# Attention and mixture of experts on one core: rebuilding the attention stage (casting loads, crossbar transposes, a softmax laid out by 32x32 block transposes)

## The chip, the cores and the metric

The kernel runs on one core of a Trainium2 chip. The core has a matrix engine (PE, with its weight loads shown apart as PEld), a vector engine (DVE), a scalar engine (ACT), a general engine (POOL) and a queue engine (SP) that only issues transfers; SP, ACT and POOL each have a queue from which transfers (DMAs) can be issued, and all transfers share 16 DMA engines. The metric is the device time of one execution in microseconds (us). All engines work through their own instructions in the order in which the program lists them.

## The reference

The inputs are `x` (8 batches, 8 heads, 512 tokens, 64 features), `state` (the same with 32 states in place of the tokens), a gate matrix and the two weight matrices of eight experts, all fp32.

```python
def _attn_ref(x, state):
    scores = scale * np.matmul(x, state.transpose(0, 1, 3, 2))
    a = softmax(scores, -1)
    xread = np.matmul(a, state)
    scores2 = scale * np.matmul(state, x.transpose(0, 1, 3, 2))
    a2 = softmax(scores2, -1)
    sread = np.matmul(a2, x)
    return np.concatenate([xread, sread], axis=2)

def _moe_ref(x, w_gate, w1, w2):                 # x: 4352 rows of 512
    logits = x @ w_gate
    P = np.exp(logits - logits.max())
    for _ in range(8):                           # Sinkhorn
        P /= P.sum(1, keepdims=True) + 1e-09
        P /= P.sum(0, keepdims=True) + 1e-09
        P *= N / E
    for e in range(E):
        h = np.maximum(x @ w1[e], 0.0)
        out += P[:, e:e + 1] * (h @ w2[e])
```

So each batch needs two softmaxes of the same 512x32 score matrix per head: along the 32 states (for `xread`) and along the 512 tokens (for `sread`). Every row of the attention output then goes through all eight experts, weighted by P.

## The kernel before, in words

The 4352 rows are nine blocks: one of 512 token rows for each batch, and one of 256 rows with the state reads of all batches. `xread` is never formed: the kernel keeps the token softmax `aT` (4 heads x 32 states on 128 partitions, 512 tokens along the row), and multiplies the small projections V = state @ w1 (`project`, L225, `project_ops`, L709) with it, which gives the hidden layer of a token block directly. The ninth block uses the state reads `xsT`.

The run has two stages.

The first stage holds the attention of all batches, expert 0 for all nine blocks, the Sinkhorn loop and the first hidden layers of expert 1. Its order is not written by hand: every piece is an `Op` with a rank (a due time), a table of engines it may run on with assumed times, the ops that it follows and the buffers it takes and uses. `issue` (L48) is a list scheduler that plays these assumed times through and emits the instructions in the order that results. The due times come from `due_x` (attention unit u), `due_e` (expert 0, block bi) and `due_1` (expert 1), L354 to L356; the assumed costs of the evictions from PSUM are `EVICT16` and `EVICT32`, L358 and L359. All PSUM tiles of this stage come from one ring of eight banks.

The attention works in 16 units: batch b, and in it two groups q of four heads. For a batch, SP loads x in two transfers of 512 KB in fp32 (L444), POOL casts them to fp16 (L451; DVE and ACT for the first batch), PE transposes x against an identity (L512), and ACT or DVE copies each transposed tile out of PSUM (L516). A unit then has:

- the scores twice, once with tokens on the partitions (`psA`, eight products, L537) and once with states on the partitions (`psB`, two products, L543);
- on DVE: the two maxima (L547, L551), a scale (L554), the difference (L558), later the sum and reciprocal (L574, L575) and the normalization of the state softmax (L569, L570);
- on ACT: the two exponentials (L562, L566);
- on POOL: the normalization of the token softmax (L578);
- on PE: the transposes of both softmaxes (L599, L603), each copied out of PSUM by ACT or DVE (L606, L609), and the state reads (L622), copied out in two pieces (L629).

`bdT` holds the transposed states in fp16, in block-diagonal form, prepared from eight small copies (L402) and 16 transposes (L416). The gate product of a block (L648) follows its attention. When all gates are done, the Sinkhorn loop (L669 to L703) runs as a chain of small DVE instructions and one PE product in each of eight rounds. Expert 0 has hidden products L746, their relu (L382, L384), output products L781 and their copy to `acc`. The weights of experts 0 and 1 are loaded in fp32 by SP (L473, L475) into three staging buffers, and cast by ACT or DVE (L480, L482).

The second stage (L875 on) is written by hand: experts 1 to 7, nine blocks each, with the output layer of one block (`layer2`, seven products of a Strassen scheme, L298, and adds on DVE, L312) mixed with the hidden layer of the next (`layer1`, L252 and L271). The weights of the next expert are loaded by SP and cast by ACT, one piece for every sixth step (`load_w`, L159).

Of the kernel before, what the change touches and what calls it, by code (L numbers as in the profile page):

```python
# [35 lines left out]
class Op:  # L36
# [3 lines left out]
    def __init__(self, rank, on, emit, after=(), takes=(), uses=()):  # L40
        self.rank, self.on, self.emit = rank, on, emit
        self.after = [d for d in after if d is not None]
        self.takes, self.end = list(takes), None
        for slot in list(takes) + list(uses):
            slot.users.append(self)


def issue(ops):  # L48
# [8 lines left out]
    while ready:  # L57
        best = None
        for op in ready:
            at = max([d.end for d in op.after], default=0.0)  # L60
            for slot in op.takes:
                t = slot.ring.free_at()
                at = None if at is None or t is None else max(at, t)
            if at is None:
                continue
            for eng, (busy, late) in op.on.items():
                start = max(at, free.get(eng, 0.0))
                key = (round(start, 2), op.rank, start + late)
                if best is None or key < best[0]:
                    best = (key, op, eng, start, busy, late)  # L70
# [7 lines left out]
        free[eng] = start + busy  # L78
        op.end = start + late
# [8 lines left out]
def kernel(  # L88
# [37 lines left out]
        tc.tile_pool(name="psum", bufs=8, space=bass.MemoryType.PSUM))}  # L126
# [13 lines left out]
    make_identity(nc, ident32)  # L140
    ones128 = persist.tile([128, 128], FP32, name="ones128")
    nc.vector.memset(ones128, 1.0)
    wg_st = persist.tile([128, NKC, E], FP32, name="wg_st")
    wgh = persist.tile([128, NKC, E], FP16, name="wgh")
    bdT = persist.tile([128, B, NQ, 128], FP16, name="bdT")
# [8 lines left out]
    mwst = ctx.enter_context(tc.tile_pool(name="moe_wst", bufs=3))  # L154
# [4 lines left out]
    def load_w(e, engines):  # L159

        w1h = mw.tile([128, NKC, F], FP16, name="w1h", tag="w1h")
        w2h = mw.tile([128, NFB, Dm], FP16, name="w2h", tag="w2h")
        w16[e] = (w1h, w2h)
        casts = []
        n = NKC + NFB // 2
        for k in range(n + 2):
            if k < n:
                if k < NKC:
                    st = mwst.tile([128, F], FP32, name="w1st", tag="wst")
                    nc.sync.dma_start(out=st, in_=w1r[e, :, k, :])  # L170
                    casts.append((w1h[:, k, :], st))
                else:
                    g = k - NKC
                    st = mwst.tile([128, 2, Dm], FP32, name="w2st", tag="wst")
                    nc.sync.dma_start(out=st, in_=w2r[e, :, ds(g * 2, 2), :])
                    casts.append((w2h[:, ds(g * 2, 2), :], st))
            if k >= 2:
                dst, src = casts[k - 2]
                eng = engines[(k - 2) % len(engines)]
                if eng is nc.scalar:  # L180
                    nc.scalar.copy(out=dst, in_=src)  # L181
                else:
                    eng.tensor_copy(out=dst, in_=src)
            yield
        if e:

            while not tpool:
                yield
            T = tpool[0].tile([128, 4, NJ, DH], FP16, name="T", tag="T")
            tsum[e] = T  # L190
            b11, b12 = w2h[:, :NJ, :DH], w2h[:, :NJ, DH:]
            b21, b22 = w2h[:, NJ:, :DH], w2h[:, NJ:, DH:]
            for i, (p, q) in enumerate(((b12, b11), (b22, T[:, 0]), (b22, b12), (b21, T[:, 1]))):
                for g in range(2):
                    jj = ds(g * (NJ // 2), NJ // 2)
                    nc.vector.tensor_sub(T[:, i, jj], p[:, jj], q[:, jj])  # L196
                    yield
# [7 lines left out]
    axs = actx.enter_context(tc.tile_pool(name="attn_xs", bufs=2))  # L205
    axp = actx.enter_context(tc.tile_pool(name="attn_x", bufs=3))
    axt = actx.enter_context(tc.tile_pool(name="attn_xt", bufs=2))
    asb = actx.enter_context(tc.tile_pool(name="attn_sb", bufs=2))
    spl = actx.enter_context(tc.tile_pool(name="stprep", bufs=1))

    def gate(bi):
        t0, tn = blocks[bi]
        n = tn // 128
        ps = bank([128, 4, E], FP32, "gate_ps")
        for i in range(n):
            rows = ds(i * 128, 128)
            if bi < B:
                terms = [(aT[:, bi, q, rows], G[:, bi, q]) for q in range(NQ)]
            else:
                terms = [(xsT[:, kc, rows], wgh[:, kc, :]) for kc in range(NKC)]  # L220
            for k, (lhs, rhs) in enumerate(terms):
                nc.tensor.matmul(ps[:, i], lhs, rhs, start=(k == 0), stop=(k == len(terms) - 1))
        nc.scalar.copy(out=logits[:, ds(t0 // 128, n)], in_=ps[:, :n])

    def project(e, bi):  # L225
# [5 lines left out]
        for f in range(F // 512):  # L231
            cols = ds(f * 512, 512)
            ps = [bank([128, 512], FP32, "v_ps", ring[0]) for _ in range(NQ)]
            for j in range(4):
                for q in range(NQ):
                    r = ((j ^ q) % 2) * 64
                    nc.tensor.matmul(ps[q][ds(j * Ns, Ns), :], bdT[ds(r, 64), bi, q, ds(j * Ns, Ns)],  # L237
# [116 lines left out]
    due_x = lambda u: 10.0 + 5.54 * u  # L354
    due_e = lambda bi: 25.1 + 13.7 * bi
    due_1 = 150.0  # L356
    rings = {"bank": Ring(8)}
    EVICT16 = {"DVE": (0.36, 0.48), "ACT": (0.50, 0.66)}  # L358
    EVICT32 = {"ACT": (0.50, 0.66), "DVE": (0.62, 0.74)}  # L359
    engines = {"DVE": nc.vector, "ACT": nc.scalar, "POOL": nc.gpsimd}  # L360

    def op(rank, on, emit, after=(), takes=(), uses=()):
        o = Op(rank, on, emit, after, takes, uses)
# [22 lines left out]
    def dma(rank, kb, emit, after=(), takes=()):  # L386
        return op(rank, {"DMA": (kb / 330.0, kb / 330.0 + 2.2)}, lambda _: emit(), after, takes)


    st_bd = spl.tile([128, B, NQ, 128], FP16, name="st_bd")  # L390
    nc.vector.memset(st_bd, 0.0)
    st_st = spl.tile([128, B, NQ, D], FP32, name="st_st")
    bd = []
    for q in range(NQ):
        for j in range(4):
# [5 lines left out]
            def place(eng, q=q, j=j):  # L401
                copy(eng, st_bd[ds(j * Ns, Ns), :, q, ds(((j ^ q) % 2) * D, D)],  # L402
                     st_st[ds(j * Ns, Ns), :, q])

            bd.append(op((0, 0), {"DVE": (0.30, 0.40), "POOL": (0.70, 0.80)}, place,
                         [dma((0, 0), 120, load)]))
# [3 lines left out]
    bdT_ready = []  # L410
    for g in range(4):
        ps = psum([128, 4, 128], FP16, "stT_ps")

        def turn(_, g=g, ps=ps):
            for i in range(4):
                nc.tensor.transpose(ps.tile[:, i], st_bd[:, 2 * g + i // 2, i % 2, :], identh)  # L416

        def keep(eng, g=g, ps=ps):
            copy(eng, bdT[:, ds(2 * g, 2)].rearrange("p b q c -> p (b q) c"), ps.tile)

        t = op((0, 1, g), {"PE": (0.35, 0.55)}, turn, bd, [ps])
        bdT_ready.append(op((0, 1, g), EVICT16, keep, [t], uses=[ps]))
    gps = psum([128, B, NQ, E], FP32, "G_ps")

    def gmul(_):
        for b in range(B):
            for q in range(NQ):
                for par in range(2):
                    nc.tensor.matmul(gps.tile[ds(par * 64, 64), b, q], bdT[:, b, q, ds(par * 64, 64)],
                                     wgh[:, 2 * q + par])  # L430

    gm_op = op((20.0,), {"PE": (1.0, 1.2)}, gmul, bdT_ready + [wgc], [gps])
    G_ready = op((20.0,), {"DVE": (0.2, 0.3), "ACT": (0.3, 0.4)},
                 lambda eng: copy(eng, G, gps.tile), [gm_op], uses=[gps])


    xn = [slot(axp, 3, [128, NSC, H, D], FP16, "x_nat") for _ in range(B)]
    x_ready = []
    for b in range(B):
        for g in range(2):  # L440
            st = slot(axs, 2, [128, H // 2, NSC * D], FP32, "x_st")

            def load(b=b, g=g, st=st):
                nc.sync.dma_start(  # L444
                    out=st.tile,
                    in_=x[b, ds(g * 4, 4), :, :].rearrange("h (p sc) d -> p h (sc d)", sc=NSC))

            def cast(eng, b=b, g=g, st=st):
                src = st.tile.rearrange("p h (sc d) -> p sc h d", sc=NSC)
                for sc in range(NSC):  # L450
                    copy(eng, xn[b].tile[:, sc, ds(g * 4, 4), :], src[:, sc])  # L451

            d = dma((0 if b < 1 else due_x(2 * b - 2), b, 0), 512, load, takes=[st])
            on = {"DVE": (0.90, 1.10), "ACT": (1.35, 1.50)} if b == 0 else {"POOL": (1.65, 1.80)}
            x_ready.append(op((0, 3) if b == 0 else (due_x(2 * b - 2),), on, cast, [d] + x_ready[2 * b:],
                              [xn[b]] if g == 0 else [], [st] + ([xn[b]] if g else [])))
# [6 lines left out]
    def weights_ops(e, rank, on):  # L463
# [3 lines left out]
        for k in range(NKC + NFB // 2):  # L467
            first = k < NKC
            st = slot(mwst, 3, [128, F], FP32, "wst")

            def load(k=k, st=st):
                if k < NKC:
                    nc.sync.dma_start(out=st.tile, in_=w1r[e, :, k, :])  # L473
                else:
                    nc.sync.dma_start(out=st.tile.rearrange("p (a b) -> p a b", a=2),  # L475
                                      in_=w2r[e, :, ds((k - NKC) * 2, 2), :])

            def cast(eng, k=k, st=st):
                if k < NKC:
# [455 lines left out]
```

## Time and profile before

| what | value |
|---|---|
| time, median of 3 runs (lowest, highest) | 793.67 us (792.33, 793.72) |
| span of the profiled execution, first to last instruction | 792.9 us |
| what the median lies above that span | 0.8 us (the profile gives no other time for its own execution) |
| PE busy | 764.5 us (96%) |
| DVE busy | 648.8 us (82%) |
| ACT busy | 566.7 us (71%) |
| POOL busy | 39.5 us (5%) |
| moved by DMA | 52.46 MB |

"Busy" is the time in which an instruction of the engine is under way. For PE it is not the same as work at full rate, since products are pipelined and their ends are modelled: what a run of products really costs is read from the start of one group to the start of the next. The same holds for DVE and ACT in a smaller measure: a DVE instruction that reads 512 fp32 values lasts 0.68 us, and the next one starts 0.60 us after it.

### The profile page before, as it was taken

To read this page: it belongs to the slowest core of one execution; us is meant where nothing else is said; L and a number is where in the kernel's file an instruction comes from. 1 tells how busy PE (TensorE), PEld (TensorE's weight loads), DVE (VectorE), ACT (ScalarE), POOL (GpSimd) and SP (SyncE) were. 2 spreads that over 40 slices of the span, in tenths; PEclk is the share of its full clock that TensorE was granted. 3 is DMA by queue.
4 is the path that set the end of the run, shared out by engine and by line. 5 is a ranking of instruction groups with operands and counts; after the bars stand their busy time and mean duration, and the time that the engine had idled before them with its cause. 6 is when DMAs were issued, how large, how long until landed. Compare 5 with 4: busy or idle time off the path is not lost.

```text
span 792.9 us, 16564 instructions
## 1 busy us (share of the span) xinstructions
PE 764.5 (96%) x6593; PEld 514.2 (65%) x6593; DVE 648.8 (82%) x1603; ACT 566.7 (71%) x1072; POOL 39.5 (5%) x80
## 2 busy tenths in 40 slices
PE   4899999989999999999999999999999999999996
PEld 3455554556667666766667666766667766767675
DVE  7898877787898888978788888978788888978885
ACT  5787776568977688577866688578866688576662
POOL 1543210000000000000000000000000000000000
PEclk9999999999999999999999999999999999999999
DMA  8874000002400033001410033001400030002233
GB/s 280 288 253 138 1 2 1 1 1 64 125 28 1 1 104 111 1 2 54 129 33 2 1 107 107 1 2 54 133 28 2 1 107 28 1 24 97 95 107 134
DMA packets 29535, 52.46 MB, mean 66 GB/s; under 512 B 4625, under 2 KB 12817, under 8 KB 29457
## 3 DMA queue, kind: packets, MB, share of 16 engines
q1 hardware_dynamic: 28368, 51.14, 20.3%
q8 instruction: 51, 0.84, 0.4%
q10 hardware_dynamic: 1088, 0.26, 0.2%
q14 instruction: 28, 0.22, 0.1%
HBM read 42.48 MB, written 8.91 MB: 65 GB/s over the span
## 4 chain that ended last, share of the span: by engine, by line
PE 63%; DVE 4%; ACT 2%; issue 0%; DVEq 0%
PE hps L252 22%; PE Bseed L298 16%; PE E L298 11%; PE A L298 10%; PE v_ps L237 3%; DVE acc L312 2%; ACT Hm L271 2%; DVE sm L277 1%; ACT w2h L181 1%; DVE sm L280 0%; DVE Hm L278 0%; DVE T L196 0%; DVE sm L279 0%; ACT w1h L181 0%; DVE acc L320 0%
## 5 line engine op out<-in xcount | busy, mean ns | idle before, releaser
L271 ACT ACTIVATE Hm<-hps 128x512 f16<-128x512 f32 (+1 forms) x488 | 262.3, 575 | 149.8 <-PE hps L252 138.9
L298 PEld LDWEIGHTS <-Hm 128*128 128x128 f16 x1904 | 185.4, 98 | 74.4 <-issue 3.9
L252 PE MATMUL hps<-aT,V 128*128 128x512 f16 x864 | 230.5, 379 | 0.0
L312 DVE SCALAR_TENSOR_TENSOR acc<-Bseed,Pmat,acc 128x256 f32<-128x256 f32 x357 | 156.9, 479 | 57.1 <-PE Bseed L298 53.6
L298 PEld LDWEIGHTS <-sm 128*128 128x128 f16 x1428 | 134.4, 98 | 54.9 <-DVE sm L277 24.4
L298 PE MATMUL Bseed<-T,Hm 128*128 128x256 f16 x952 | 124.5, 273 | 2.7 <-DVE acc L312 2.5
L298 PE MATMUL A<-w2h,Hm 128*128 128x256 f16 x952 | 126.1, 273 | 0.5
L252 PEld LDWEIGHTS <-V 128*128 128x128 f16 x864 | 84.5, 98 | 44.4
L241 ACT CAST V<-v_ps 128x512 f16<-128x512 f32 x216 | 111.0, 608 | 0.0
L312 DVE SCALAR_TENSOR_TENSOR acc<-E,Pmat,acc 128x256 f32<-128x256 f32 x238 | 104.4, 478 | 5.4 <-PE E L298 1.0
L277 DVE TENSOR_TENSOR sm<-Hm 128x512 f16<-128x512 f16 (+1 forms) x122 | 49.9, 409 | 21.6 <-ACT Hm L271 20.8
L298 PE MATMUL E<-T,sm 128*128 128x256 f16 x476 | 64.4, 274 | 0.7
L781 PE MATMUL yps<-w2h,hT 128*128 128x512 f16 x272 | 64.6, 379 | 0.0
L312 DVE SCALAR_TENSOR_TENSOR acc<-A,Pmat,acc 128x256 f32<-128x256 f32 x119 | 52.4, 479 | 15.0 <-PE A L298 14.9
L298 PE MATMUL Bseed<-T,sm 128*128 128x256 f16 x476 | 62.3, 272 | 2.3 <-ACT Bseed L323 2.3
L298 PE MATMUL E<-w2h,sm 128*128 128x256 f16 x476 | 62.3, 273 | 0.0
L278 DVE TENSOR_TENSOR Hm<-Hm 128x512 f16<-128x512 f16 (+1 forms) x122 | 50.0, 410 | 4.2
L280 DVE TENSOR_TENSOR sm<-Hm,sm 128x512 f16<-128x512 f16 (+1 forms) x122 | 50.0, 410 | 4.2
L279 DVE TENSOR_TENSOR sm<-sm,Hm 128x512 f16<-128x512 f16 (+1 forms) x122 | 49.1, 403 | 0.0
L323 ACT COPY Bseed<-A 128x512 f32<-128x512 f32 (+1 forms) x63 | 34.7, 552 | 18.7 <-PE A L298 15.6
L781 PEld LDWEIGHTS <-hT 128*128 128x128 f16 x272 | 24.8, 98 | 27.5 <-issue 2.6
L746 PE MATMUL hps<-aT,V 128*128 128x512 f16 x160 | 41.1, 389 | 0.4
(114 smaller groups left out, 626.1 us busy)
## 6 DMA issues: line engine op xcount, KB each, us to landing
w1st<-in_moe_w_dram SPq DMA_DIRECT2D x24, 512.0 KB, 3.6
w2st<-in_moe_w_dram SPq DMA_DIRECT2D x24, 512.0 KB, 3.6
x_st<-in_x_dram SPq DMA_DIRECT2D x16, 512.0 KB, 5.1
wst<-in_moe_w_dram SPq DMA_DIRECT2D x16, 512.0 KB, 6.1
out_dram<-acc SPq DMA_DIRECT2D x32, 256.0 KB, 3.1
out_dram<-acc SPq DMA_DIRECT2D x8, 64.0 KB, 1.7
st_st<-in_state_dram ACTq DMA_DIRECT2D x4, 64.0 KB, 3.2
st_st<-in_state_dram SPq DMA_DIRECT2D x4, 64.0 KB, 3.0
```

Of the source, the lines that this page charges most:

```text
L241: nc.scalar.copy(out=V[:, q, cols], in_=ps[q])
L252: nc.tensor.matmul(out, lhs, rhs, start=(k == 0), stop=(k == len(terms) - 1))
L271: nc.scalar.activation(out=Hm[:, i, j, :tn], in_=hps[:, :tn], func=AF.Relu)
L277: nc.vector.tensor_add(s1, a21, a22)
L278: nc.vector.tensor_sub(a21, a11, a21)
L279: nc.vector.tensor_sub(s2, s1, a11)
L280: nc.vector.tensor_sub(s4, a12, s2)
L298: nc.tensor.matmul(dst[:, c], lhs(j, c), rhs[:, j], start=first and c == 0 and j == 0, stop=(j == NJ - 1), skip_group_check=True)
L312: nc.vector.scalar_tensor_tensor(out=dst, in0=src[:, c], scalar=p[:, k], in1=dst, op0=ALU.mult, op1=ALU.add)
L323: nc.scalar.copy(out=Bb[:, :nk], in_=A[:, :nk])
L746: nc.tensor.matmul(ps.tile[:, :tn], lhs, rhs, start=(k == 0), stop=(k == len(terms) - 1))
L781: nc.tensor.matmul(yps.tile, hT[fb].tile[:, ds(tk * 128, 128)], w2h[:, fb, :], start=(fb == 0), stop=(fb == NFB - 1))
```

## The change

The attention stage is rebuilt, and the weight loads of the whole kernel change their way.

- **Loads.** x and all expert weights are loaded by DMAs issued from POOL that cast from fp32 to fp16 on the way. The staging buffers and all cast instructions on POOL, ACT and DVE go. The eight loads of `state` stay on SP and ACT, in fp32.
- **Transposed x.** A DMA issued from SP, `dma_start_transpose`, writes the transposed fp16 x of one group of four heads (128 partitions x 1024 values) into `xT`: two a batch. The PE transposes of x and their copies go.
- **One score product.** The scores are formed once, with states on the partitions: eight products on 64x32 tiles of the PE array, 256 columns each, into two PSUM banks of their own (a ring with one place). The other ring has six banks instead of eight.
- **Token softmax.** DVE's `transpose`, which transposes 32x32 blocks, turns the scores into a layout with the 32 states of one token along the row. Maximum, difference, exponential, sum and normalization work there, all but the exponential on DVE, and a second block transpose turns the result into `aT` with no PE transpose and no copy out of PSUM. POOL's normalization goes to DVE.
- **State reads.** 16 products on 128x64 tiles instead of eight, copied out in one piece instead of two.
- **Prepared states.** Two copies instead of eight and a memset; the gate matrix G takes 64 small products on tiles instead of 32.
- **Planner.** New due times and costs; an op can occupy a second engine (`also`), and an alternative can carry a handicap (`SHY`, 0.8 us for fp32 evictions on DVE).

The core of the diff:

```diff
-    def load_w(e, engines):
+    def load_w(e):
...
-                    st = mwst.tile([128, F], FP32, name="w1st", tag="wst")
-                    nc.sync.dma_start(out=st, in_=w1r[e, :, k, :])
-                    casts.append((w1h[:, k, :], st))
...
+        for g in range(2):
+            nc.gpsimd.dma_start(out=w1h[:, ds(2 * g, 2), :], in_=w1r[e, :, ds(2 * g, 2), :])
+        for g in range(2):
+            nc.gpsimd.dma_start(out=w2h[:, ds(NJ * g, NJ), :], in_=w2r[e, :, ds(NJ * g, NJ), :])
+        for _ in range(10):
             yield
...
-    due_x = lambda u: 10.0 + 5.54 * u
-    due_e = lambda bi: 25.1 + 13.7 * bi
-    due_1 = 150.0
-    rings = {"bank": Ring(8)}
-    EVICT16 = {"DVE": (0.36, 0.48), "ACT": (0.50, 0.66)}
-    EVICT32 = {"ACT": (0.50, 0.66), "DVE": (0.62, 0.74)}
+    due_x = lambda u: 6.0 + 4.4 * u
+    due_e = lambda bi: 14.0 + 13.0 * bi
+    due_1 = 135.0
+    rings = {"bank": Ring(6), "pair": Ring(1)}
+    SHY = 0.8
+    EVICT16 = {"DVE": (0.34, 0.48), "ACT": (0.48, 0.66)}
+    EVICT32 = {"ACT": (0.48, 0.66), "DVE": (0.60, 0.74, SHY)}
...
+    xn = [slot(axp, 4, [128, H, NSC * D], FP16, "x_nat") for _ in range(B)]
+    for b in range(B):
+        def load(b=b):
+            for g in range(2):
+                nc.gpsimd.dma_start(
+                    out=xn[b].tile[:, ds(g * 4, 4), :],
+                    in_=x[b, ds(g * 4, 4), :, :].rearrange("h (p sc) d -> p h (sc d)", sc=NSC))
+
+        x_ready.append(dma((0, 1 + 2 * b), 1024, load, takes=[xn[b]], also={"POOL": 2.0}))
...
-    weights_ops(0, (3.0, 4), {"ACT": (0.95, 1.10), "DVE": (0.75, 0.95)})
-    weights_ops(1, (due_1 - 30.0, 0), {"ACT": (0.95, 1.10), "DVE": (0.75, 0.95)})
+    weights_ops(0, [(0, 2), (0, 4)])
+    weights_ops(1, [(due_1 - 60.0, k) for k in range(2)])
...
-                    nc.tensor.transpose(ps.tile[:, ds(sc * 128, 128)],
-                                        xn[b].tile[:, sc, ds(2 * hp, 2), :], identh)
...
+        xT = slot(axt, 3, [128, H * NSC // 2, 128], FP16, "xT")
+        for g in range(2):
+            def turn(b=b, g=g, xT=xT):
+                nc.sync.dma_start_transpose(out=xT.tile[:, ds(8 * g, 8), :],
+                                            in_=xn[b].tile[:, ds(4 * g, 4), :].rearrange("p h c -> p (h c)"))
...
+            def score(_, b=b, q=q, xT=xT, ps=ps):
+                for j in range(4):
+                    for s_ in range(2):
+                        nc.tensor.matmul(ps.tile[ds(j * Ns, Ns), s_, :S // 2],
+                                         stT[ds(s_ * 64, 64), b, q, ds(j * Ns, Ns)],
+                                         xT.tile[ds(s_ * 64, 64), ds(q * 8 + (j ^ q) * 2, 2), :],
+                                         tile_position=(s_ * 64, j * Ns))
...
+            def flip(_, ps=ps, eA=eA):
+                nc.vector.transpose(out=tokens(eA.tile.rearrange("p k n -> p (k n)")), in_=scores(ps))
+
+            def maxA(_, eA=eA, mxA=mxA):
+                nc.vector.reduce_max(out=mxA.tile, in_=eA.tile, axis=AX_X)
...
+            def flipA(_, b=b, q=q, a16=a16):
+                nc.vector.transpose(out=aT[:, b, q], in_=a16.tile.rearrange("p k n -> p (k n)"))
...
-            g1 = op(r(7), {"POOL": (1.00, 1.15)}, normA, [f1], [a16], [eA, rA, sA])
+            g1 = op(r(7), {"DVE": (0.60, 0.72)}, normA, [f1], [a16],
+                    [eA, rA, sA])
+            a_ready[b, q] = op(r(8), {"DVE": (0.60, 0.75)}, flipA, [g1], [], [a16])
...
-            def turnA(_, a16=a16, pa=pa):
-                for sc in range(NSC):
-                    nc.tensor.transpose(pa.tile[:, sc], a16.tile[:, sc], identh)
...
+                for sc in range(NSC):
+                    for par in range(2):
+                        for i in range(2):
+                            hl = 2 * par + i
+                            nc.tensor.matmul(su.tile[ds(i * 64, 64), par],
+                                             xn[b].tile[:, 4 * q + hl, ds(sc * D, D)],
+                                             ETs.tile[:, sc, ds((hl ^ q) * Ns, Ns)],
+                                             start=(sc == 0 and par == 0), stop=(sc == NSC - 1),
+                                             tile_position=(0, i * 64), skip_group_check=True)
```

## The prediction

> **What bounds the kernel now.** First I cut the span where its character changes, with the busy time of each engine in each stretch: at the first hidden product of expert 0 (24.7 us), the end of attention (119.5), the first product of the hand-written stage (165.5) and the last product (787.2).
>
> ```profile
> core 0: us, PE busy (x) PEld busy (x) DVE busy (x) ACT busy (x) POOL busy (x), PEclk, DMA share, GB/s
> 0.00:24.70 24.70, 13.07 (x165) 8.99 (x166) 18.59 (x46) 14.32 (x27) 6.05 (x18) 1.00 0.88 275
> 24.70:119.50 94.80, 91.67 (x873) 49.22 (x878) 79.85 (x187) 72.10 (x155) 33.44 (x62) 0.98 0.38 129
> 119.50:165.50 46.00, 44.22 (x286) 21.81 (x287) 35.73 (x97) 30.47 (x62) 0.00 (x0) 1.00 0.00 1
> 165.50:787.20 621.70, 615.50 (x5285) 434.16 (x5284) 514.18 (x1275) 449.84 (x832) 0.00 (x0) 1.00 0.17 53
> ```
>
> The second column is the stretch, then come busy times. From 24.7 us on PE is idle for 4.9 us in the first stage (3.1 + 1.8) and 6.2 us in the second; only the first 24.7 us have much (11.6 us), while x arrives. So PE bounds both stages, and what the change is worth is the PE work that it takes out of the first stage, unless another engine takes over. DVE and ACT together are busy for 77% of two engines between 24.7 and 165.5 us (218.2 of 281.6).
>
> What a PE group costs is read from the timeline of PE, start to next start (first column), not from the length (second):
>
> ```profile
> 62.80 0.61 PE L512 MATMUL xT_ps<-identh,x_nat 128*128 128x128 f16 x8
> 63.24 1.03 PE L746 MATMUL hps<-aT,V 128*128 128x512 f16 x4
> ...
> 65.31 0.40 PE L622 MATMUL su_ps<-ETs,x_nat 128*128 128x64 f16 x8
> 65.54 0.59 PE L746 MATMUL hps<-aT,V 128*128 128x512 f16 x2
> ...
> 70.39 0.41 PE L722 MATMUL v_ps<-w1h,bdT 64*32 64x512 f16 x8
> 70.74 1.04 PE L781 MATMUL yps<-w2h,hT 128*128 128x512 f16 x4
> 71.61 0.39 PE L599 MATMUL ET_ps<-identh,E 128*128 128x128 f16 x4
> 71.83 0.40 PE L537 MATMUL psA<-bdT,xT 128*128 128x64 f16 x8
> 72.16 0.41 PE L543 MATMUL psB<-xT,bdT 128*64 128x512 f16 x2
> 72.50 0.40 PE L603 MATMUL aT_ps<-identh,a 128*128 128x128 f16 x4
> 72.73 0.40 PE L622 MATMUL su_ps<-ETs,x_nat 128*128 128x64 f16 x8
> ```
>
> So the eight transposes of x for a unit cost 0.44 us, `psA` 0.33, `psB` 0.34, the transposes of `a` 0.23, the state reads 0.23. On DVE the same reading of its timeline gives 0.60 us for each pass over 512 fp32 values, though each lasts 0.68:
>
> ```profile
> 98.75 0.68 DVE L547 TENSOR_REDUCE mxA<-psA 128x16 f32<-128x512 f32 x1
> 99.37 0.69 DVE L551 TENSOR_REDUCE nmB<-psB 128x1 f32<-128x512 f32 x1
> 99.98 0.68 DVE L558 TENSOR_TENSOR eA<-psA,mxA 128x512 f32<-128x512 f32 x1
> 100.58 0.14 DVE L554 TENSOR_SCALAR nsB<-nmB 128x1 f32<-128x1 f32 x1
> ```
>
> And the rows for transfers, with the median time to landing last:
>
> ```profile
> x_st<-in_x_dram SPq DMA_DIRECT2D x16, 512.0 KB, 5.1
> wst<-in_moe_w_dram SPq DMA_DIRECT2D x16, 512.0 KB, 6.1
> out_dram<-acc SPq DMA_DIRECT2D x32, 256.0 KB, 3.1
> ```
>
> **The change, part by part.**
>
> *PE work of a unit.* Removed: 0.44 (x) + 0.33 + 0.34 (both scores) + 0.23 (transposes of `a`) = 1.34 us. Added: the single score product. Nearest is L722, eight products on 64x32 tiles with 512 columns in 0.35 us; the score has the same tiles and half the columns, so between 0.17 and 0.35, and I take 0.25, half the columns and a switch of the tiling. The state reads become 16 products of half the width: between no dearer and twice 0.23; I take 0.12 more. Net saving 0.97 a unit (0.76 to 1.17). In the stretch from 24.7 to 119.5 us the trace has 104 products of `psA`, 13 units: **-12.6 us** (-9.9 to -15.2). The units ahead of it run while PE waits anyway. G takes 64 products instead of 32 (1.0 us now, so up to 2 us); they lie in the first 20 us, hidden by PE's own waits there.
>
> *Start of expert 0.* It needs both units of batch 0 and w1. Now: x transfers issued at 3.5 us behind the state loads of SP, cast at 8.2, first score at 11.0, first hidden product at 24.7. After: POOL issues x after its identity (ends at 1.3 us now); two pieces, by the 5.1 us row and with some sharing, land at about 7.5. Then the transposition, 256 KB. The trace has no transfer that transposes, and none issued from POOL or with a cast. By the rows it lands in 3.1 us (256 KB alone) to 6.1 (weights, queue full), and the weights do stream then; I take 4: score at 11.5, as now. Then two units on DVE (below, 4.85 us each) with the exponentials of ACT between: about 11 us, where it took 13.7 with casts, copies and POOL's turn (1.1 us each) in the way. First hidden product at 22.5: **-2.2 us** (-4.7 if transfers are as good as alone; +3.3 if a transposition takes 6.1 and x shares its way with w1). PE idles in this stretch, so its saved work gains nothing there.
>
> *DVE and ACT.* Per unit DVE gains the first block transpose (0.60 by the fp32 rows, below by the 0.33 spacing of an fp16 copy, above by twice the row, 1.2), the normalization (0.60 by L558) and the second transpose, fp16 (0.33 to 0.60, I take 0.40): +1.6. DVE's own part now is 3.25 a unit (0.60+0.61+0.60+0.15, sum and reciprocal 0.88, normalization 0.41), after 4.85. Off DVE and ACT come two copies of x (0.50 on ACT, 0.34 on DVE; 0.86 for the pair), the copy of `aT` (0.43) and half of the `xsT` copy (0.24): -1.53. That is even. The casts of weights still to come after 24.7 us are nine, about 8 us in all. So 211 us of work in 128 us of stretch, 82% of two engines, against 77%. In the 10 us pieces of the trace where the two were 89 to 90% busy (40 to 60 us) PE was busy 9.2 to 9.8; I add **+2 us** of PE waits (-2, if the casts and copies are what made it wait; +6, PE waiting 8% of the time).
>
> *PSUM.* The ring falls from eight banks to six, but its users `psA`, `psB`, the x and the `a` transposes go: nothing. If evictions fall behind, this is the +6 above.
>
> *Queues.* On SP only transpositions stand behind a waiting transposition, and then stores from 711 us on: nothing. On POOL, x of batch 4 waits until batch 0 frees its place (about 25 us), and behind it stand x 5 to 7 and expert 1's weights, 4 MB or 15 us at 275 GB/s; needed at about 145, hidden by 100 us. The fewer preparations of `state` (3.56 us of casts and a 0.91 us memset on DVE) hide behind x's arrival.
>
> *Second stage.* The 48 casts of `load_w` (1.04 us each on ACT) go. PE hardly waits: a block takes 10.23 us from one `E` group to its like, and 10.46 where a cast meets the relu (289.28 to 299.74). One or two such blocks an expert, six loads: **-2.1 us** (0 to -3). The four loads of an expert are issued at once in block 1, 66 steps of some 15 a block ahead of the sums on DVE that read them first, 4.4 blocks or 45 us; that covers 4.2 MB down to 93 GB/s.
>
> *Sum.* -2.2 - 12.6 + 2 = -12.8 in the first stage (ends at 152.7), -2.1 in the second: -14.9. Span 792.9 - 14.9 = 778.0; the median stood 0.8 above the span, so 779. By the ends of the terms: -24.6 to -0.6, 769 to 793.
>
> **Rivals.** *A, slower: the transposition is the pace.* All 16 go through SP's queue, one for each unit. From the last score to 165.5 us there are now 53.9 us (rest of the unit, gates, Sinkhorn loop). If one takes P, the stage ends at 8 + 16 P + 53.9; with 2.1 us gained later it decides from P = 6.6 us on. At 8 us it ends at 190: 816. For it: nothing here shows the rate of such a transfer. Against: 6.6 is above the slowest row with twice the bytes. The Trainium skill speaks for this rival in "VectorE: DVE Perf Modes", section "The three transpose paths": a 128x128 block takes 1309 ns by crossbar against 390 ns on TensorE; eight blocks one after another would be an estimated 10.5 us a transposition, and the formula would end at 230 us, near 856. Its page "DMA: Bandwidth & Descriptors", section "Latency and other measured facts", has 261 GB/s, by which 256 KB are an estimated 1.0 us and the rival doesn't arise; no run here shows either yet.
>
> *B, slower: the casting loads run at half rate.* w2 of expert 0 is fourth on POOL: 6.8 MB with the state come first or with it. At 275 GB/s it is there at 27 us, before the first output product of now (31.9). At half, at 50; from there about 121 us of PE work remain (133.6 now, less 10.7 saved and 4 done in the meantime, plus 2): end at 171, 797. It decides below some 150 GB/s. Against: the bytes read are the same as now, those written half.
>
> *C, less gain: DVE sets the attention's pace.* Now a unit takes 6.7 us (first score 11.0, last 111.6). With 4.85 forced on DVE and pace 5.7, DVE has 0.85 us a unit for everything else. If the block transposes cost twice their row, DVE needs 6 us a unit and the pace stays near 6.3: the Sinkhorn loop, which must follow, ends the stage at about 160, and the time is 786 to 788.
>
> **How the numbers follow.** My forecast 0.62, C 0.20, A 0.09, B 0.06, something in the second stage or elsewhere 0.03. About 0.2% is what a measurement here can tell from no change. Forecast and C are faster by more than that, but for their upper ends (0.03), and B ends 0.4% above: faster 0.80, same 0.03, slower 0.17. The range runs from 766, a little past the lower sum, to 795: above it lie A, B and the rest, below some 0.03.
>
> **What would show it.** Right: no L512 or `aT_ps` groups, score groups near 0.25 us, first expert 0 product at 22 to 23 us, first `layer2` product near 153, PE idle 7 us between. Wrong if a transposition lands later than 6 us, if PE's waits after 25 us name DVE, or if `yps` waits for a load.

## The result, and the profile after

| | before | after |
|---|---|---|
| time, median (lowest, highest) | 793.52 us (792.33, 793.72), 4 runs | 788.26 us (786.92, 788.79), 4 runs |
| profiled execution: span | 792.9 us | 786.8 us |
| profiled execution: own time | not listed | 788.79 us |

The ratio of the times is 0.9933, with a 95% interval of 0.9917 to 0.9949. The change gains 5.3 us, where 14.5 us were forecast. Between the two profiled spans the gain is 6.1 us.

Cut at the same four events as before (first hidden product, end of attention, first product of the hand-written stage, last product), the profile of the changed kernel reads as follows. The columns are the stretch, its length and the busy times of the engines.

```profile
core 0: us, PE busy (x) PEld busy (x) DVE busy (x) ACT busy (x) POOL busy (x), PEclk, DMA share, GB/s
0.00:33.30 33.30, 9.68 (x192) 5.53 (x192) 12.68 (x30) 10.65 (x21) 10.69 (x22) 1.00 1.18 170
33.30:118.00 84.70, 81.00 (x784) 37.25 (x781) 75.03 (x176) 68.51 (x148) 8.83 (x12) 0.98 0.82 90
118.00:164.50 46.50, 44.38 (x280) 22.10 (x273) 31.60 (x87) 33.86 (x69) 2.88 (x4) 1.00 0.28 46
164.50:780.90 616.40, 614.03 (x5284) 434.73 (x5283) 512.51 (x1271) 410.95 (x784) 14.42 (x20) 1.00 0.15 32
```

The first stretch has grown from 24.7 to 33.3 us, and PE is idle in 23.6 us of it. The rest has shrunk: from the first hidden product to the first product of the hand-written stage it was 140.7 us and is 131.2. By starts of product groups (24.74, 165.46 and 786.60 us before; 33.33, 164.50 and 780.07 after) the balance is:

| stretch | forecast | measured |
|---|---|---|
| up to the first hidden product | -2.2 | +8.6 |
| from there to the hand-written stage | -10.6 | -9.6 |
| the hand-written stage, to its last product | -2.1 | -5.6 |
| last product to the end | 0 | +0.4 |
| sum, of the spans | -14.9 | -6.1 |

PE's timeline shows where the first stretch goes (start, length, group; the brackets hold the idle time ahead of the group and what ended it).

```profile
18.57 0.41 PE L469 MATMUL psB<-xT,stT 64*32 64x256 f16 x8 [7.05 <-DMA xT<-x_nat]
25.49 0.41 PE L469 MATMUL psB<-xT,stT 64*32 64x256 f16 x8 [6.50 <-DMA xT<-x_nat]
...
33.33 0.61 PE L684 MATMUL hps<-aT,V 128*128 128x512 f16 x1
...
71.52 0.30 PE L469 MATMUL psB<-xT,stT 64*32 64x256 f16 x8
71.75 1.04 PE L719 MATMUL yps<-w2h,hT 128*128 128x512 f16 x4
...
73.81 0.43 PE L562 MATMUL su_ps<-ETs,x_nat 128*64 128x32 f16 x16
74.17 1.90 PE L719 MATMUL yps<-w2h,hT 128*128 128x512 f16 x8
```

The first two score groups wait 7.05 and 6.50 us, both for transposed x. Once the stage runs, a score costs 0.23 us from its start to the next (71.52 to 71.75) and the state reads 0.36 (73.81 to 74.17). In the list of waits of PE up to 170 us, a transposition is named only in these two (us in total, times, longest):

```profile
PE psB L469 <- DMA xT<-x_nat: 13.5, 2, 7.0
```

The list of transfers gives the median time from issue to landing last. For the transpositions it is 12.0 us, for all 16; the shortest took 4.3 and the longest 17.2.

```profile
xT<-x_nat SPq DMA_TRANSPOSE x16, 12.0
```

The first transposition is issued at 7.63 us and its score starts at 18.57, so it took 10.9 us. Two answers on the transfers, for 8 to 12 us and for 12 to 18 us, show why. q0 carries the casting loads from POOL, q1 what SP issues; the numbers are packets, megabytes written and the time of the packets as a share of the 16 DMA engines.

```profile
q0 software_dynamic: 465, 0.77, 111.4%
q1 hardware_dynamic: 10, 0.00, 0.5%
...
q0 software_dynamic: 1157, 0.81, 89.7%
q1 hardware_dynamic: 1151, 0.29, 39.8%
```

In the first four microseconds after its issue almost nothing of the transposition moves, while the loads fill the DMA engines. Then its 1024 packets of 256 bytes go one for one with packets of the loads (1151 against 1157, packets of 4 bytes among them). By the packets' own records the first moves 3.9 us after the issue and the last 6.0 us later.

On DVE the same reading by starts as before gives 0.63 us for the second block transpose; the first costs 0.64 in the same way (56.53 to 57.17).

```profile
54.88 0.70 DVE L528 STREAM_TRANSPOSE aT<-a 128x512 f16<-128x512 f16 x1
55.51 0.65 DVE L504 TENSOR_TENSOR eA<-eA,mxA 128x512 f32<-128x512 f32 x1
```

### The profile page after: what moved, and what is told of

The parts are those of the page before. It is cut to its first block, busy times and chain, and to the rows that moved or that the text cites. A ratio compares the mean times of both kernels' runs of the same rounds, so it can differ in the third digit from the quotient of the medians.

```text
span 786.8 us, 16245 instructions
## 1 busy us (share of the span) xinstructions
PE 749.1 (95%) x6529; PEld 499.6 (64%) x6529; DVE 632.1 (80%) x1561; ACT 524.0 (67%) x1020; POOL 36.8 (5%) x58
## 3 DMA queue, kind: packets, MB, share of 16 engines
q0 software_dynamic: 21248, 20.97, 18.1%
## 4 chain that ended last, share of the span: by engine, by line
PE 66%; DVE 4%; ACT 1%; issue 0%; DVEq 0%
PE hps L219 23%; PE Bseed L265 17%; PE E L265 11%; PE A L265 11%; PE v_ps L204 3%; DVE acc L279 2%; DVE sm L244 1%; ACT Hm L238 1%; DVE sm L247 0%; DVE Hm L245 0%; DVE T L178 0%; DVE sm L246 0%; DVE acc L287 0%; ACT Bseed L290 0%; DVEq L279 0%
## 5 line engine op out<-in xcount | busy, mean ns | idle before, releaser
L265 PE MATMUL A<-w2h,Hm 128*128 128x256 f16 x952 | 124.5, 273 | 1.9 <-ACT Hm L350 1.9
L719 PE MATMUL yps<-w2h,hT 128*128 128x512 f16 x272 | 67.3, 386 | 0.0
L279 DVE SCALAR_TENSOR_TENSOR acc<-A,Pmat,acc 128x256 f32<-128x256 f32 x119 | 52.3, 479 | 15.0 <-PE A L265 14.9
L719 PEld LDWEIGHTS <-hT 128*128 128x128 f16 x272 | 24.9, 100 | 26.8 <-issue 2.9
```

Of the source, the lines that this page charges most:

```text
L265: nc.tensor.matmul(dst[:, c], lhs(j, c), rhs[:, j], start=first and c == 0 and j == 0, stop=(j == NJ - 1), skip_group_check=True)
L279: nc.vector.scalar_tensor_tensor(out=dst, in0=src[:, c], scalar=p[:, k], in1=dst, op0=ALU.mult, op1=ALU.add)
L719: nc.tensor.matmul(yps.tile, hT[fb].tile[:, ds(tk * 128, 128)], w2h[:, fb, :], start=(fb == 0), stop=(fb == NFB - 1))
```

## The experiments

Three theories went into the first runs. S, sharing: the first two transpositions are late because they share the DMA engines with the loads of weights and of the next x, and the gain that was forecast is lost there. R, own rate: a transposition of 256 KB takes some 7 to 11 us whatever runs beside it. D: the late start is no loss, since the attention runs at a pace that something else sets, and the time stays as it is.

**The first transpositions alone.** POOL reads a column of each transposed tile of batch 0 before it issues any other load, so the DMA engines hold nothing else meanwhile.

```diff
+            def wait_xt(_):
+                for g in range(2):
+                    nc.gpsimd.tensor_copy(out=hold_t[:, ds(g, 1)], in_=xT0.tile[:, 8 * g + 7, 0:1])
+            held = [op((0, 1), {"POOL": (0.1, 0.2)}, wait_xt, xt0, [], [xT0])]
...
-        x_ready.append(dma((0, 1 + 2 * b), 1024, load, takes=[xn[b]], also={"POOL": 2.0}))
+        x_ready.append(dma((0, 1 + 2 * b), 1024, load, held, takes=[xn[b]], also={"POOL": 2.0}))
...
-            w_ready[e, k] = dma(rank[k], 2048, load, [], [w], [], {"POOL": 2.0})
+            w_ready[e, k] = dma(rank[k], 2048, load, held, [w], [], {"POOL": 2.0})
```

> The changed kernel, but POOL reads one column of batch 0's two transposed tiles before it issues any load except x of batch 0, so the first two transpositions have the DMA engines to themselves. Theory S (sharing): a transposition is slow because its packets take turns with those of the casting loads queued with it. Then the first two land within 5 us of their issue at about 7.6 us (10.9 now), first score near 12.5 us (18.6 now), second score near 15 to 17 (25.5 now), first hidden product of expert 0 near 25 to 27 us (33.3 now; w1 now comes later), time 780 to 785 us (changed kernel 788.3). Rival R (own rate): a transposition takes some 7 us by itself. Then the second score stays 7 us behind the first, the first hidden product stays at 31 or later with the weights later too, time 789 to 794. Rival D (the end of the stage hangs on DVE's attention and the Sinkhorn loop, not on when PE starts expert 0): the start moves, the time stays at 788.

Measured: 782.5 us (781.85 to 784.83), ratio to before 0.9859 (0.9839 to 0.9879), 5.8 us below the changed kernel. The transfers of this kernel between 8 and 12 us, first the queues, then the two transpositions issued in that time:

```profile
q1 hardware_dynamic: 2023, 0.51, 66.4%
q0 software_dynamic: 90, 0.04, 8.1%
...
xT<-x_nat SPq DMA_TRANSPOSE x2, 3.2
```

And its PE timeline:

```profile
11.52 0.41 PE L486 MATMUL psB<-xT,stT 64*32 64x256 f16 x8 [0.51 <-DMA xT<-x_nat]
...
25.55 4.57 PE L701 MATMUL hps<-aT,V 128*128 128x512 f16 x16
32.22 0.30 PE L486 MATMUL psB<-xT,stT 64*32 64x256 f16 x8 [2.11 <-DMA xT<-x_nat]
```

With the engines free, the two transpositions land in 3.2 us in the middle (0.51 MB written between 8 and 12 us), the first score starts at 11.52 instead of 18.57, and the first hidden product at 25.55 instead of 33.33. R falls, and so does D. Of the 7.8 us that the start gains, 5.8 reach the end: x of the next batch, held back, is now late for the third and fourth unit (2.11 and, at 36.58 us, 3.41), and those transpositions meet the weights in their turn (median of all 16: 7.4 us).

**Batch 0, or batches 0 and 1, transposed on PE.** The transposes go through PSUM in four tiles a batch, with a copy of each, as the kernel before did it; the other batches keep the crossbar. `NPE` is the number of such batches.

```diff
+            if b < NPE:
...
+                    def turnx(_, b=b, g=g, h=h, pt=pt):
+                        src = xn[b].tile[:, ds(4 * g + 2 * h, 2), :].rearrange("p h c -> p (h c)")
+                        for i in range(4):
+                            nc.tensor.transpose(pt.tile[:, i], src[:, ds(i * 128, 128)], identh)
...
+                    def keepx(eng, g=g, h=h, pt=pt, xT=xT):
+                        copy(eng, xT.tile[:, ds(8 * g + 4 * h, 4), :], pt.tile)
...
+                continue
```

> The changed kernel, but x of batch 0 is transposed on PE (16 transposes, four copies out of PSUM), batches 1 to 7 by the crossbar. If the late start is what ate the gain: first score near 10 us, first hidden product near 22 us, and the first stage ends 6 to 11 us earlier: 778 to 783 us; toward the upper end if the crossbar transposition of batch 1, which still shares the engines with the loads, holds the third unit until 30 us. Rival D (start of expert 0 does not matter): 787 to 789.

> The same with batches 0 and 1 transposed on PE. If sharing at the start is the whole loss: first hidden product near 22 us, third unit's score near 20 us, 776 to 780 us, 2 to 3 us better than with batch 0 alone. Rival: batch 1's transposition is hidden behind the work of batch 0, then no better than with batch 0 alone. Rival D: 787 to 789.

With one batch: 784.85 us (781.04 to 785.87), ratio 0.9871 (0.9838 to 0.9903). That is above the 778 to 783 us expected: four score groups still wait for the crossbar, 6.8 us in all. The PE timeline of this kernel shows the wait move to the third score, the first that needs the crossbar (the first is at 11.90 us, the first hidden product at 26.18):

```profile
25.83 0.41 PE L493 MATMUL psB<-xT,stT 64*32 64x256 f16 x8 [3.08 <-DMA xT<-x_nat]
```

With two batches: 779.7 us (777.16 to 787.47), ratio 0.9835 (0.9778 to 0.9891). Its timeline, from the fastest of its four executions, starts near the forecast:

```profile
11.91 0.45 PE L493 MATMUL psB<-xT,stT 64*32 64x256 f16 x8
...
24.14 1.17 PE L708 MATMUL hps<-aT,V 128*128 128x512 f16 x4
...
153.32 1.03 PE L265 MATMUL A<-w2h,Hm 128*128 128x256 f16 x8 [1.92 <-ACT Hm L350]
```

The first hidden product is at 24.14 us and the hand-written stage starts at 153.32 (forecast: 22.5 and 153). Between the two lie 129.2 us, where the sum had 130.2, so this part of the forecast holds once the start is mended. The time is 8.6 us less than that of the changed kernel, though PE transposes two batches again. The scatter of this kernel is wide, and it was run again below.

**All batches on PE.** No transposition by the crossbar is left.

```diff
-    NPE = 2
+    NPE = 8
```

> The same with all batches transposed on PE, no crossbar at all. PE gets 0.44 us a unit back (13 units after the start: 5.7 us) and ACT or DVE two copies a unit (0.86 us): by the sum of the prediction 5 to 8 us slower than with two batches on PE, 782 to 787 us. If PE and the copying engines have room that the sum does not see, within 2 us of it.

Measured: 781.88 us (780.94 to 783.27), ratio 0.9847 (0.9829 to 0.9866). The interval overlaps that of two batches, so these two can't be told apart, and the 5 to 8 us that the sum put on it don't show; but the kernel without the crossbar is 6 us faster than the changed one, which uses it throughout. For the first batches, then, the crossbar costs more than all 16 transpositions save on PE.

**The casts of the second stage alone.** The kernel before, with nothing changed but `load_w`: the weights of experts 2 to 7 come by casting DMAs.

```diff
-                    st = mwst.tile([128, F], FP32, name="w1st", tag="wst")
-                    nc.sync.dma_start(out=st, in_=w1r[e, :, k, :])
...
+        for g in range(2):
+            nc.gpsimd.dma_start(out=w1h[:, ds(2 * g, 2), :], in_=w1r[e, :, ds(2 * g, 2), :])
+        for g in range(2):
+            nc.gpsimd.dma_start(out=w2h[:, ds(NJ * g, NJ), :], in_=w2r[e, :, ds(NJ * g, NJ), :])
+        for _ in range(10):
             yield
```

> The kernel before, with one part of the change alone: in the second stage the next expert's weights come by casting loads from POOL, with no staging and no casts on ACT; the attention stage is untouched. In the changed kernel the second stage is 5.3 us shorter (616.4 against 621.7). If the casts on ACT are what it loses there: about 3.7 us from the steady part (blocks of 10.46 us become 10.23), so 789 to 791 us where the kernel before has 793.6. Rival: the gain of the second stage comes from how the first stage leaves it (its first block), then 793 and no change. Rival: loads from POOL disturb DVE or PE: slower.

Measured: 790.11 us (789.98 to 790.27), ratio 0.9956 (0.9942 to 0.9969): 3.9 us less than the 794.01 of before beside it. On PE's timeline of this kernel the second projection of the hand-written stage and its last group start at

```profile
174.30 0.63 PE L222 MATMUL v_ps<-w1h,bdT 64*32 64x512 f16 x16
...
781.60 0.60 PE L283 MATMUL Bseed<-T,Hm 128*128 128x256 f16 x4
```

From the second projection to the last group that is 607.30 us; the same stretch is 611.15 us in the kernel before (175.45 to 786.60) and 607.25 in the changed one (172.82 to 780.07). So the casts that left ACT are worth 3.9 us, and nothing else in that stretch is worth anything. The other 1.67 us of the stage lie in its first block (9.99 us before and here, where it starts at 164.31; 8.32 after the change), where PE waited 1.84 us for sums on DVE and now waits 0.17. Some 0.9 us of that are not gained: the changed kernel waits 1.92 us for `Hm` just ahead of the stage, where it waited 1.01.

**Two batches on PE, once more.** The same kernel again (`e6_pe2again`; `e3_pe2` is its first set of runs).

> The same kernel as e3_pe2, for its spread (777.2, 777.6, 781.8, 787.5). If the spread is the granted clock: times follow the mean clock of the run (0.999 gives 777, 0.985 gives 782 to 788). If it is the order in which transpositions and loads meet on the queues, the runs spread at the same clock too.

Measured: 780.66 us (778.84 to 781.37), ratio 0.9833 (0.9817 to 0.985). The ratio of the first time holds, and its interval is narrower. The four times don't follow the clock: 778.84 us at 0.991, 780.41 and 781.37 at 0.992, 780.91 at 0.988.

**Where the later transpositions matter.** Two edits of that kernel: the weights of expert 1 behind all loads of x, or four batches on PE.

```diff
-            w_ready[e, k] = dma(rank[k], 2048, load, [], [w], [], {"POOL": 2.0})
+            w_ready[e, k] = dma(rank[k], 2048, load, x_ready if e else [], [w], [], {"POOL": 2.0})
```

```diff
-    NPE = 2
+    NPE = 4
```

> e3_pe2 with the loads of expert 1's weights behind all loads of x, so no casting load of weights shares the DMA engines with the transpositions of batches 4 to 7 any more. If sharing later in the stage still costs: 1 to 3 us better than e6_pe2again and a smaller spread. If these transpositions are hidden (PE names one wait of 1.5 us for them in e3_pe2): the same within 1 us.

> Batches 0 to 3 transposed on PE, 4 to 7 by the crossbar. By PE's own work 0.44 us a unit more than with two batches, four units: 1.8 us slower than e6_pe2again; less, or faster, if the transpositions of batches 2 and 3, which share the engines with the first loads, still make PE wait.

Late weights: 777.37 us (775.21 to 778.95), ratio 0.9793 (0.9772 to 0.9815). Four batches on PE: 776.06 us (775.07 to 776.81), ratio 0.9778 (0.9763 to 0.9793). The 11 transpositions issued between 26 and 110 us land in 11.6 us in the middle in the kernel run again, and in 3.6 us in the one with late weights. PE's waits for transposed x are 4.1 us in three waits in the kernel run again:

```profile
PE psB L493 <- DMA xT<-x_nat: 4.1, 3, 2.3
```

They fall on the scores at 45.48, 52.17 and 59.41 us, of batches 3 and 4, and no such wait is in PE's list in either edit. So each edit takes away the same rest of the cost by another way; the times fall by 3 to 5 us. That four batches on PE would cost more than two, by the 0.44 us a unit, was wrong: the waits that go are worth more. The waits alone, less 1.8 us of PE work, would give 2.3 us of the 4.6; where the rest comes from stays open.

**Both edits together, and late weights alone.** The first is a try for the fastest version, the second a test of S: in the changed kernel itself, late weights of expert 1 leave what shares with the first two transpositions as it is.

> Batches 0 to 3 transposed on PE, 4 to 7 by the crossbar, and the weights of expert 1 behind all loads of x: the two edits of the runs before together. If late weights gain because transpositions land sooner (3.4 us in the middle against 9.5, and PE's waits for xT gone), this gains 0 to 1 us over the kernel with four batches on PE, whose PE no longer waits for xT: 775 to 776. If they gain by the order that the planner finds with them, by the same 3 us as before: 773. Slower than 777 would mean that neither holds.

> The changed kernel with one edit: the weights of expert 1 go behind all loads of x. What shares the DMA engines with the first two transpositions (7.6 to 25.4 us) are x of the next batches and the weights of expert 0, which stay. Theory of sharing at the start: first score within 1 us of 18.6, first hidden product within 2 us of 33.3, time 786 to 788, the later transpositions faster but unseen. If the loads of the whole first stage held the kernel back instead: 3 us gained or more, 785 or below.

Together: 776.06 us (774.77 to 776.48), ratio 0.9776 (0.9763 to 0.979), the same as four batches on PE alone. The second edit finds nothing more to gain, as it must if both remove the same waits. The granted clock isn't what gains: at a mean of 0.990 to 0.992 this kernel takes 775.9 to 776.5 us, and the kernel with two batches, run again, takes 778.8 to 781.4 at 0.991 and 0.992. Late weights alone: 788.41 us (786.66 to 788.84), ratio 0.9932 (0.9918 to 0.9946), the time of the changed kernel. Its transpositions land in 7.3 us in the middle, and still its PE timeline starts the same way:

```profile
18.29 0.41 PE L469 MATMUL psB<-xT,stT 64*32 64x256 f16 x8 [7.22 <-DMA xT<-x_nat]
...
33.02 0.39 PE L684 MATMUL hps<-aT,V 128*128 128x512 f16 x1
```

In the changed kernel only the first two transpositions cost time. The others may be slow or fast without its showing, because the late start has put the rest behind them.

The version with four batches on PE, with or without late weights, is 17 to 18 us faster than the kernel before and 12 us faster than the changed one.

## Why the prediction was wrong

**The step that failed: "Start of expert 0", and in it the 4 us for a transposition.** It was bounded by 3.1 us (256 KB alone) and 6.1 (weights with the queue full). x landed when the prediction said (7.5; the first transposition, which waits for it, is issued at 7.63). The transposition then took 10.9 us, and the second landed 6.9 us behind the first, so the two units took 14.8 us from first score to first hidden product instead of 11. (Not all of these 3.8 us are the transposition's: with batches 0 and 1 transposed on PE the same stretch is 12.2 us, 11.91 to 24.14, so the 11 was about 1.2 short.) Together that is 33.3 instead of 22.5: 10.8 us, more than the whole miss of 9.3. The lower bound was right: alone, two land in 3.2 us. The upper bound was not, because the row it came from is a transfer among its like, of the same packets in the same queue. A transposition moves in packets of 256 bytes, and beside loads each of them waited for one of theirs; 1024 of them took 6.0 us, against 1.4 us in the kernel where they ran alone. The Trainium skill says in "DMA: Bandwidth & Descriptors", section "Queues, rings and completion order", that each engine goes round robin between the queue rows that it has work for, a packet at a time. The trace agrees in the stretch from 12 to 18 us, with 1157 packets to 1151, and the loads' packets are the larger ones (0.81 MB to 0.29). By the Trainium skill's same section a packet typically holds 9 to 17 descriptors; whether the packets that the profile counts are the same thing, no run shows. What the 3.9 us before the first packet are made of stays open: with free engines the first packet moved 1.3 us after the issue, and no run took this delay apart.

**Right, in mechanism and size: PE work and pace.** The score was costed at 0.25 us and is 0.23 to 0.24, the state reads at 0.35 and are 0.36. From the first hidden product to the hand-written stage the sum was -12.6 + 2 = -10.6, and it is -9.6. DVE and ACT are busy for 80% of their time there (209.0 of 262.4 us; forecast 82%), and PE is idle for 5.8 us of 131.2 (forecast 7). The kernels with a mended start take 126.8 to 133.6 us for this part, around the 130.1 that the sum makes of it, and start the hand-written stage at 151.0 to 159.5 us: 151 to 153 with four batches on PE and in the first profile with two, 155 to 159.5 in the others.

**Mis-sized without effect: the second block transpose.** It was taken as 0.40 us, by an fp16 copy, and costs 0.63, about the same as on fp32 and just past the end of its range (0.60). DVE's forced work is 5.1 us a unit, not 4.85. The pace, 5.7 us a unit (18.6 to 104.5 us for 15 units), hides it.

**Mis-sized: the second stage.** Forecast -2.1 (0 to -3), measured -5.6. The casts account for 3.9 of it, as the run with `load_w` alone shows, so the count of one or two blocks an expert that a cast delays by 0.23 us was too small: 0.65 us an expert. The other 1.7 us are the wait that shrank in its first block, of which 0.9 came back as a wait ahead of the stage.

**The last 0.8 us.** The prediction put 0.8 us between span and time. In the runs that list both, the time is 1.7 to 2.1 us above the span (788.79 to 786.8). By that the profiled execution of before was an estimated 1.1 to 1.5 us slower than its median, that of the changed kernel 0.5 (788.79 to 788.26), and 6.1 us between the spans agree with 5.3 between the medians. The fast ends of the prediction's terms add up to -24.9 and not to -24.6; its 769 stays.

**The rivals.** A, the transposition as the pace, was right on its mechanism in one place: the second transposition landed 6.9 us after the first, above the 6.6 us from which it decides. It held for these two alone; the later ones landed 0.8 to 13 us apart, before a stage that took 5.7 us a unit needed them, and PE did not wait for one of them. The Trainium skill's 1309 ns a block ("VectorE: DVE Perf Modes", section "The three transpose paths") gave an estimated 10.5 us for eight blocks in a row; measured alone, eight blocks landed in 3.2 us, so the blocks don't follow one another at that price, and the 10.9 us have another cause. B, casting loads at half rate, fell: q0 wrote 20.97 MB in 18.1% of the span, 147 GB/s, which is 295 GB/s read, against 318 for the loads and stores of before (51.14 MB in 20.3%). The last of w2 of expert 0 landed at 26.5 us, where the prediction had 27 at the full rate and 50 at half, and no `yps` waited for a load. C, DVE as the pace, fell with the pace of 5.7: its 786 to 788 us lie next to the measured 788.26 by luck, since the block transposes cost 0.63 and not the 1.2 on which C rested. Of the three signs named as fatal, "a transposition lands later than 6 us" came true. By its letter "if PE's waits after 25 us name DVE" did too, but for 2.3 us of the listed waits between the first hidden product and the hand-written stage, against 2.5 before.

## What to carry to other kernels

A transfer at the head of the critical chain must be costed beside what is issued around it, by its packets and not by its bytes: here the queue with the small packets moved as many of them as the queue with the large ones, and so got the small share of the rate. Let the first transfers of a kernel run alone, or take them off the DMA engines: where the changed kernel gained 5 us, the first gained 11, and the second, for four batches, 17 to 18. In the changed kernel the later transpositions cost nothing, because a stage of work hid them behind the late start; with the start mended they made PE wait again, until they were taken off the DMA engines too or the bulk loads were queued behind them. All bulk loads of these kernels cast, and no run put a transposition beside loads that don't.

## What the runs showed of the hardware

- **Block transposes on DVE** cost nearly the same for fp16, read from SBUF, and fp32, read from PSUM: the 16 of each took 700 and 709 ns on average.

```profile
L490 DVE STREAM_TRANSPOSE eA<-psB 128x512 f32<-128x512 f32 x16 | 11.3, 709 | 11.9 <-PE psB L469 11.8
L528 DVE STREAM_TRANSPOSE aT<-a 128x512 f16<-128x512 f16 x16 | 11.2, 700 | 0.0
```

- **TensorE's granted clock** falls to half in stretches of 3.41, 6.83 or 13.65 us. The kernel before and the changed one have one of 3.41 us each in their records before the end, that with batch 0 alone on PE has three of 13.7 us in all, and the fastest execution of two batches on PE (777.16 us) has none. In the first set of runs with two batches the time goes with the mean clock: 777.16 us at 0.999, 777.64 at 0.994, 781.76 and 787.47 at 0.986 and 0.985. The last two differ by 5.7 us at nearly the same clock, so the clock is not all of the scatter. In the two profiles of this kernel the waits for transposed x differ as well: one of 1.5 us in the execution of 777.16 us, three of 4.1 us in all in that of 781.37. The rest was not found.
